# Whole key tiles for a sliding-window block and the first chunk of a memory-augmented attention, with a third token-major buffer

## The chip, the cores and the metric

The kernel runs on one core of one Trainium2 chip. Time is device microseconds of one execution; of several executions the median is taken. The core has five engines that run their own instruction streams and wait for one another through semaphores: TensorE (PE in the profile, its weight loads PEld), VectorE (DVE), ScalarE (ACT), GpSimd (POOL) and SyncE (SP), which here only issues DMAs. Each engine works its instructions in the order in which they were written.

## The reference

Two attentions on different inputs of 2048 tokens with 640 features, 32 heads of 20; the outputs stand side by side (2048 x 1280).

```python
# A: four segments of 512 tokens, in order, with a memory (M, z)
logits = q_s @ k_s.T * scale + mask           # causal inside the segment
a_dot  = softmax(logits) @ v_s
a_mem  = (phi(q_s) @ M) / (phi(q_s) @ z + 1e-6)   # phi(t) = t+1 if t>0 else exp(t)
o      = g * a_mem + (1-g) * a_dot            # g = sigmoid(beta), per head
M, z   = M + phi(k_s).T @ v_s, z + sum(phi(k_s))
A      = concat(o) @ wo_A
# B: sliding window: key j counts for query i when 0 <= i-j < 256
B      = (softmax(where(window, q @ k.T * scale, -1e9)) @ v) @ wo_B
out    = concat([A, B], -1)
```

## The kernel before

Both attentions are cut into four chunks of 512 tokens, and the eight chunks run in the order A0, B0, A1, B1, ..., B3, numbered n = 0 to 7. The 32 heads stand in eight groups g of four, the heads of a group in four bands of 32 partitions. A chunk is worked in two halves of four groups; `phases` (L1067) pairs the first half of one chunk with the second half of the one before.

For each chunk, `qk_job` (L405) projects queries and keys, writes them to a scratch in device memory and reads them back spread out by heads; `v_job` (L593) projects the values, token-major, 21 columns a head of which the last is one, so that the value product yields the softmax's denominator too. `pq_job` and `pk_job` make phi of q and k for the memory through `phi` (L437): one exponential on ACT and two operations on DVE for each group of 128 rows. `dm_job` updates the memory.

Scores are made in batches (`score_batch`, L680). A batch is up to 512 columns of queries for each of a group's four heads, with 128 keys on the partitions, in two banks of PSUM. An entry (kt, b0, nb, c0) means: key tile kt, against nb query blocks of 64 from block b0, at column c0. Two exponentials on ACT (L725) turn the two banks into the probability tile `pt` (six buffers, `NPT`). Where a key tile lies on the edge of the window, a mask follows: `mask` (L761) on GpSimd with an affine select, "diag" for the causal edge (L775) and "far" for the window's far edge (L771).

Before the change a diagonal is cut finer than a key tile: the tables `MAIN_A`, `MAIN_B` and `MAIN_B0` (L60 to L65) hold the whole tiles, and a further "half" batch pairs 64 keys with 64 queries (L692 to L710), two such squares stacked on the 128 partitions. Its mask is one DVE operation, `mask_half` (L748, L756). For the value product of such a half, the values of the other 64 keys must be zero: `v_job` copies half tiles of the values by DMA into the zero-padded tiles `vtop` and `vbot` (`vz`, L633 to L653; for the last half in the room of kA and qA, cleared by `clear_spare`). Per pair of groups A has four main batches of 512 columns and a half batch of 256. B has, per pair, four of 512 and a half batch of 512; in B's first chunk two of the main batches have 256. In the last chunk (n = 7) `unit` (L939) goes by query tile i: two batches of 512 and a half batch of 256 for each i and half.

The value product (`av`, L780) gathers a group's result of all queries in one PSUM bank of two; `turn` transposes it on DVE (L812), `norm` (L816) divides by the denominator (L835, L830) into the token-major tile `o` of the chunk (two buffers, L1301). `back_job` (L872) transposes `o` on DVE (L867) into `oD` (two buffers), after the output of chunk n-2 is done; `final_job` (L890) multiplies oD by the output weights, per 128 tokens in two pieces of 320 columns (L905), and stores 640 columns by a DMA (L919). In A's later chunks a second result, that of the memory, is added to o on GpSimd (L848).

The order of all of it is written out by a planner when the kernel is built. `Flow` (L75) keeps an estimated clock for each engine. The loop in `body` (L1158) takes, at each point, the next score batch if its inputs and banks are there, else a value product that is ready, else a projection job, and last an output projection (`fins`). A chunk's first value product asks that the tile `o` be free: `done.get((n-2, "oD"))` (L1206, L1211, L1227). `ORDER` holds a number for each batch that breaks ties, `SHIFT` how the two halves of a phase interleave, `T_W` when the first weights are expected. `evac` (L216) decides for each PSUM bank whether ACT (L224) or DVE (L226) copies it out: ACT if its estimated end lies before that of DVE less `EDGE`.

Of the kernel before, what the change touches and what calls it, by code (L numbers as in the profile page):

```python
# [9 lines left out]
ALU = mybir.AluOpType  # L10
# [3 lines left out]
P = 128  # L14
# [14 lines left out]
    713, 960, 766, 330, 869, 772, 401, 0, 661, 621, 0, 421, 799, 434, 873, 66, 0, 0, 682, 989,  # L29
    286, 308, 0, 611, 753, 150, 129, 90, 788, 0, 206, 866, 667, 116, 549, 871, 639, 130, 0, 0,  # L30
    912, 958, 43, 481, 0, 273, 464, 759, 0, 576, 75, 116, 453, 298, 776, 822, 0, 592, 326, 352,
    83, 232, 230, 0, 831, 0, 447, 297, 432, 523, 968, 587, 614, 386, 789, 692, 822, 229, 935,
    581, 834, 344, 0, 0, 113, 0, 549, 887, 906, 0, 610, 0, 343, 660, 0, 585, 0, 505, 0, 324, 0,
    71, 0, 0, 0, 312, 359, 655, 958, 400, 526, 773, 865, 950, 534, 3, 0, 753, 384, 394, 707,
    67, 758, 381, 953, 225, 83, 144, 0, 183, 598, 460, 507, 727, 0, 122, 0, 0, 568, 356, 711,
    739, 632, 0, 572, 339, 542, 0, 276, 229, 0, 0, 278, 631, 350, 717, 0, 0, 325, 609, 541,
    789, 0, 15, 479, 188, 0, 0, 688, 196, 403, 0, 956, 270,
)
STRETCH = 1
EDGE = -300.0  # L40
# [5 lines left out]
T_W = (5600.0, 7200.0, 10500.0, 12500.0, 14500.0, 16500.0)  # L46
SLACK = 500.0
SPREAD = 500.0
SHIFT = (0.0, 1.0, 0.75, 1.0, -0.5, 0.25, -1.0, 0.0, 0.0)
PKT = (2000.0, 2100.0, 1000.0)  # L50
NU = 2
SPREAD_NS = 400.0
# [13 lines left out]


# [122 lines left out]
class _K:  # L190
# [53 lines left out]
    def consts_rows(self):  # L244
# [17 lines left out]
        for kind, sides in (("A", ((0, -1, 0), (64, -1, 0))), ("B", ((0, -1, 0), (64, 1, -1)))):  # L262
# [174 lines left out]
    def phi(self, out, x, ready, then):  # L437

        nc, f = self.nc, self.f
        e = self.wk.tile([P, L], BF16, name="e", bufs=2)  # L440
        nc.scalar.activation(out=e[:], in_=x, func=ACT.Exp)  # L441
        ta = f.on_act(519.0, ready)

        def s1():
            nc.vector.tensor_scalar(out=out, in0=x, scalar1=1.0, scalar2=1.0,
                                    op0=ALU.add, op1=ALU.max)
            f.on_dve(150.0, 0.0, True)

        def s2():
            nc.vector.tensor_tensor(out=out, in0=out, in1=e[:], op=ALU.min)  # L450
            f.on_dve(345.0, 0.0, True)
# [4 lines left out]
    def phi_all(self, pieces, then):  # L456
# [6 lines left out]
        for x, (o_, i_) in enumerate(pieces):  # L463
            while len(ends) < x - 1:
                yield self.f.pe + 200.0
            if x > 1:
                yield ends[x - 2]

            def fin(x=x):
# [953 lines left out]
```

## Time and profile before

| what | value |
|---|---|
| median of 8 runs | 360.04 us (355.71 to 362.17) |
| the profiled execution | 360.22 us |
| its span, first to last instruction | 358.5 us |
| TensorE clock granted, mean | 0.995 |
| busy: PE, DVE, ACT, POOL | 332.9, 296.1, 316.7, 153.6 us |
| exponentials of scores (L725) | 328, of which 264 with 1024 elements and 64 with 512 |
| masks on GpSimd (L771, L775) | 184, each of 512 elements, 128.0 us |
| DMA engines busy on the main queue | 47.5% of the span |

How to read it: busy time of an engine is the union of its instructions' spans; since ACT's and PE's instructions overlap, the mean duration of one times their count is more than the busy time. In a row of instructions, the first number after the line and shapes is busy time, the second the mean in ns of one, and what follows is the idle time just before them with what ended it. In a timeline row the first two numbers are start and length in us. In a table of stretches each engine has its busy us and its count of instructions. The chain of waits is followed back from the last instruction.

### The profile page before, as it was taken

What the parts mean: (1) busy time and instruction counts of PE and PEld (TensorE: products, weight loads), DVE (VectorE), ACT (ScalarE), POOL (GpSimd) and SP (SyncE); (2) the same over time, 40 slices, a digit from 0 to 9 for tenths busy, and PEclk for the clock granted to TensorE, in tenths of its full rate; (3) what the DMA queues carried; (4) which work ended last, traced back from release to release, by engine and by line L of the source; (5) the groups of instructions that cost most, each with busy time, mean ns of one, the idle gap of its engine ahead of it and who ended that gap; (6) DMA issues with size and microseconds to landing.
All of it is one profiled execution on the core that took longest, in us unless ns stands there. A gap on an engine that the chain in (4) does not pass through costs nothing.

```text
span 358.5 us, 17793 instructions
## 1 busy us (share of the span) xinstructions
PE 332.9 (93%) x7732; PEld 184.6 (51%) x7732; DVE 296.1 (83%) x607; ACT 316.7 (88%) x406; POOL 153.6 (43%) x243
## 2 busy tenths in 40 slices
PE   8799999999999999999899989979999999989896
PEld 3345545454445544565645445645565545656564
DVE  7567878599999899988897997299898899898784
ACT  2586996699999999999999999679999999999892
POOL 8120222243246434565337256015664356545641
PEclk9899999999999999999999999999999999999999
DMA  7994784356775641557665332562335323211012
GB/s 224 386 407 145 188 147 135 121 162 168 239 168 152 174 123 58 164 150 144 210 189 146 93 90 82 176 168 58 108 110 176 94 74 121 79 59 57 23 60 75
DMA packets 43350, 51.12 MB, mean 143 GB/s; under 512 B 12984, under 2 KB 38392, under 8 KB 43272
## 3 DMA queue, kind: packets, MB, share of 16 engines
q1 hardware_dynamic: 42696, 49.57, 47.5%
q8 instruction: 60, 0.98, 1.2%
q10 hardware_dynamic: 576, 0.42, 0.4%
q14 instruction: 18, 0.15, 0.2%
HBM read 24.91 MB, written 19.14 MB: 123 GB/s over the span
## 4 chain that ended last, share of the span: by engine, by line
PE 50%; ACT 21%; DVE 14%; issue 6%; DMA 6%; POOL 1%; ACTq 0%; SPq 0%; DVEq 0%; POOLq 0%
ACT pt L725 19%; PE m L422 17%; PE m L606 7%; PE m L789 7%; PE sc L714 7%; PE m L905 7%; DVE tt L812 4%; PE sc L704 3%; DMA wv_A<-in_A_wv_dram 2%; DVE o L830 2%; DVE st L226 2%; DMA scr_qA<-st 1%; DMA beta<-in_A_beta_dram 1%; PE m L347 1%; ACT e L441 1%
## 5 line engine op out<-in xcount | busy, mean ns | idle before, releaser
L725 ACT ACTIVATE pt<-sc 128x1024 bf16<-128x1024 f32 (+1 forms) x328 | 284.1, 981 | 16.9 <-PE sc L714 9.3
L775 POOL TENSOR_SCALAR_AFFINE_SELECT pt<-pt 128x512 bf16<-128x512 bf16 x128 | 89.1, 696 | 166.3 <-ACT pt L725 145.2
L812 DVE STREAM_TRANSPOSE tt<-m 128x512 f32<-128x512 f32 x88 | 62.0, 709 | 17.4 <-PE m L789 16.3
L771 POOL TENSOR_SCALAR_AFFINE_SELECT pt<-pt 128x512 bf16<-128x512 bf16 x56 | 38.9, 695 | 29.3 <-ACT pt L725 27.1
L226 DVE CAST st<-m 128x512 bf16<-128x512 f32 x57 | 38.9, 683 | 11.4 <-PE m L422 10.8
L606 PEld LDWEIGHTS <-xT 128*128 128x128 bf16 x400 | 32.8, 99 | 18.6 <-issue 4.9
L830 DVE TENSOR_TENSOR o<-tt,rr 128x320 bf16<-128x320 f32 x64 | 37.9, 595 | 0.9
L905 PEld LDWEIGHTS <-oD 128*128 128x128 bf16 x280 | 24.4, 97 | 19.1 <-issue 10.0
L905 PE MATMUL m<-wo_A,oD 128*128 128x320 bf16 x160 | 28.3, 300 | 3.2 <-DVE tt L812 2.1
L714 PE MATMUL sc<-qA,kA 32*128 32x64 bf16 (+3 forms) x640 | 29.3, 252 | 1.4 <-ACT pt L725 0.8
L714 PE MATMUL sc<-qB,kB 32*128 32x64 bf16 (+3 forms) x896 | 28.0, 221 | 2.7 <-issue 1.5
L606 PE MATMUL m<-wv_A,xT 128*128 128x320 bf16 (+2 forms) x200 | 27.9, 281 | 2.6 <-DMA wv_A<-in_A_wv_dram 2.4
L606 PE MATMUL m<-wBv,xT 128*128 128x320 bf16 (+2 forms) x200 | 27.4, 273 | 0.7 <-DVE tt L812 0.5
L867 DVE STREAM_TRANSPOSE oD<-o 128x512 bf16<-128x512 bf16 x35 | 22.7, 676 | 5.9 <-PE m L905 5.9
L422 PE MATMUL m<-xT,wBk 128*128 128x512 bf16 x100 | 26.3, 380 | 1.1 <-DVE tt L812 0.5
L422 PE MATMUL m<-xT,wBq 128*128 128x512 bf16 x100 | 26.2, 381 | 0.5 <-DVE tt L812 0.2
L226 DVE CAST ot<-m 128x320 bf16<-128x320 f32 x48 | 22.6, 476 | 4.5 <-PE m L905 4.3
L789 PE MATMUL m<-pt,vB 128*32 128x64 bf16 (+3 forms) x896 | 23.4, 225 | 2.0 <-ACT ot L224 1.1
L714 PEld LDWEIGHTS <-kB 32*128 32x128 bf16 x896 | 13.4, 92 | 20.2 <-issue 19.2
L422 PE MATMUL m<-xT,wk_A 128*128 128x512 bf16 x90 | 22.8, 380 | 0.9 <-DVE st L226 0.7
L422 PE MATMUL m<-xT,wq_A 128*128 128x512 bf16 x90 | 22.3, 380 | 0.8 <-DVE tt L812 0.6
L789 PE MATMUL m<-pt,vA 128*32 128x64 bf16 (+3 forms) x640 | 21.8, 253 | 1.1 <-DVE ot L226 0.9
(106 smaller groups left out, 480.2 us busy)
## 6 DMA issues: line engine op xcount, KB each, us to landing
out_dram<-ot SPq DMA_DIRECT2D x31, 160.0 KB
scr_kB<-st SPq DMA_DIRECT2D x20, 128.0 KB
scr_qB<-st SPq DMA_DIRECT2D x20, 128.0 KB
kB<-scr_kB SPq DMA_DIRECT2D x32, 80.0 KB
qB<-scr_qB SPq DMA_DIRECT2D x32, 80.0 KB
scr_kA<-st SPq DMA_DIRECT2D x18, 128.0 KB
scr_qA<-st SPq DMA_DIRECT2D x18, 128.0 KB
kA<-scr_kA SPq DMA_DIRECT2D x28, 80.0 KB
```

The lines of the kernel that those rows point to most:

```text
L226: nc.vector.tensor_copy(out=out, in_=in_)
L422: nc.tensor.matmul(ps[:, :], lhsT=w_ap[:, kt, m * P:(m + 1) * P], rhs=xT[:, kt, :], start=(kt == 0), stop=(kt == self.KT - 1))
L606: nc.tensor.matmul(ps[:, c0:c0 + w], lhsT=xT[:, kt, tt * P:(tt + 1) * P], rhs=w_ap[:, kt, a:a + w], start=(kt == 0), stop=(kt == self.KT - 1))
L714: nc.tensor.matmul(ps[j // 2][:, j % 2, c0:c0 + 64 * nb], lhsT=k[rows, g, P * kc:P * kc + P], rhs=q[rows, g, 64 * b0:64 * (b0 + nb)], star ...
L725: nc.scalar.activation(out=pt[:, 2 * i:2 * i + 2, 0:hi], in_=ps[i][:, :, 0:hi], func=ACT.Exp, scale=self.scale)
L771: nc.gpsimd.affine_select(out=blk, in_=blk, pattern=[[0, r], [-1, w]], compare_op=ALU.is_ge, fill=self.zero, base=-1, channel_multiplier=1)
L775: nc.gpsimd.affine_select(out=blk, in_=blk, pattern=[[0, r], [1, w]], compare_op=ALU.is_ge, fill=self.zero, base=128 - w, channel_multipli ...
L789: nc.tensor.matmul(O[HD * j:HD * j + HD, c:c + 64 * nb], lhsT=self.vcols(v, h // 16 if vk[0] == "v" else 0, vt, h, HD), rhs=rhs[j], start= ...
L812: self.nc.vector.transpose(out=tt[:], in_=O[:, :])
L830: nc.vector.tensor_tensor(out=out, in0=a, in1=b, op=ALU.mult)
L867: self.nc.vector.transpose(out=self.oD[n][:, x:y, b0:b0 + nb, :].rearrange("p c b t -> p b c t"), in_=o[:, b0:b0 + nb, :].rearrange("p b ( ...
L905: nc.tensor.matmul(ps[:, 0:320], lhsT=oD[:, m, :, :].rearrange("p b t -> p (b t)"), rhs=wo[:, m, cs], start=(m == 0), stop=(m == self.KT - 1))
```

## The change

Four things go together.

1. For all B chunks and for A's first chunk (`WHOLE`) the scores go by whole key tiles of 128 x 128 alone. The half batches, their DVE mask and the zero-padded value copies are left out there; masks are 128 columns wide, on GpSimd. A's chunks 1 to 3 keep their halves. The batches per pair of groups: A0 five of 512 columns; B0 four of 512 and one of 256; B1 and B2 six of 512; B3 three of 512 for each query tile and half.
2. The tiles vtop and vbot of B are gone, and `o` has three buffers; a chunk's value products wait for oD of chunk n-3.
3. `phi` takes up to three groups in one instruction (`EW`), with one buffer for the exponentials (`EB`).
4. `final_job` makes, of 512 tokens, four pieces of 128 tokens x 512 columns and one piece with the remaining 128 columns of all four, each with a store of its own; the last chunk has `last_job` with two pieces of 320 columns for each 128 tokens, each stored on its own.

With these, `EDGE` goes from -300 to 250, `T_W`'s third entry from 10500 to 12300, `SPREAD_NS` from 400 to 540, and `ORDER` and `SHIFT` have other numbers.

```diff
-EDGE = -300.0
+EW, EB = 3, 1
+EDGE = 250.0
...
-T_W = (5600.0, 7200.0, 10500.0, 12500.0, 14500.0, 16500.0)
+T_W = (5600.0, 7200.0, 12300.0, 12500.0, 14500.0, 16500.0)
...
-SHIFT = (0.0, 1.0, 0.75, 1.0, -0.5, 0.25, -1.0, 0.0, 0.0)
+SHIFT = (0.0, 0.5, 0.0, 0.25, 0.0, 0.25, 0.5, 1.0, 0.0)
...
+WHOLE = ((0, 0), (0, 1), (1, 0), (1, 1), (3, 0), (3, 1), (5, 0), (5, 1), (7, 0), (7, 1))
+WHOLE_A = [([(0, 0, 8, 0)], [("diag", 0, 0, 128)]),
+           ([(3, 6, 2, 0), (1, 2, 6, 128)], [("diag", 0, 128, 128)])]
+WHOLE_B = [([(0, 0, 6, 128), (3, 6, 2, 0)], [("diag", 0, 128, 128), ("far", 384, 0, 128)]),
+           ([(1, 2, 6, 0), (-2, 0, 2, 384)], [("diag", 0, 0, 128), ("far", 256, 128, 128)]),
+           ([(2, 4, 4, 0), (-1, 0, 4, 256)], [("diag", 0, 0, 128), ("far", 384, 0, 128)])]
+WHOLE_B0 = [([(3, 6, 2, 0), (0, 0, 6, 128)], [("diag", 0, 128, 128), ("far", 384, 0, 128)]),
+            ([(2, 4, 2, 0), (1, 2, 6, 128)], [("diag", 0, 128, 128), ("far", 384, 0, 128)])]
...
-    def phi(self, out, x, ready, then):
+    def phi(self, out, x, w, ready, then):
...
+        e = self.wk.tile([P, EW, L], BF16, name="e", bufs=EB)[:, 0:w, :]
+        nc.scalar.activation(out=e, in_=x, func=ACT.Exp)
...
+        if (n, half) not in WHOLE:
+            t = yield from self.v_copies(n, half, v, gate, t)
+        for g in range(4 * half, 4 * half + 4):
+            self.mark(t + DVE_OUT, n, "v", g)
...
+    def final_job(self, n, wo, out2d, col):
+        nc, f = self.nc, self.f
+        yield self.known(n, "oD")
+        r = self.row0[n]
+        for x in range(LT + 1):
...
+            for y, (qt, a, w) in enumerate([(x, 0, 512)] if x < LT else
+                                           [(qt, 512, P) for qt in range(LT)]):
...
+            t = self.evac(ot[:], ps[:, :], 512, 612.0)
...
+                if (n, half) in WHOLE:
+                    for g in gs[::2]:
+                        out.append([n, [(g1, (i - y, 2 * i, 2, 256 * x + 128 * (2 - y)))
+                                        for x, g1 in enumerate((g, g + 1)) for y in (2, 1)],
+                                    [("far", 0, 256, 128)], []])
+                    out.insert(1, [n, [(g, (i, 2 * i, 2, 128 * x)) for x, g in enumerate(gs)],
+                                   [("diag", 0, 256, 128), ("diag", 128, 256, 128)], []])
...
+        if (n, half) in WHOLE:
+            for g0 in gs[::2]:
+                out = []
+                for g in (g0, g0 + 1):
+                    for ent, ms in WHOLE_A if kind == "A" else WHOLE_B if c else WHOLE_B0:
+                        out.append([n, [(g, e) for e in ent], ms, []])
+                    if g > g0 or c and kind == "B":
+                        out[-1][3].append(g)
+                    elif kind == "A":
+                        out.append([n, [(g, (2, 4, 4, 0)), (g + 1, (2, 4, 4, 256))],
+                                    [("diag", 0, 256, 128)], [g]])
+                    else:
+                        out.append([n, [(g, (2, 6, 2, 0)), (g + 1, (2, 6, 2, 128))], [], [g]])
...
-                            self.done.get((n - 2, "oD")) if n > 1 else 0.0]
+                            self.done.get((n - 3, "oD")) if n > 2 else 0.0]
...
-            o_t[n] = self.big.tile([P, L // HD, GW], BF16, name="o", bufs=2)
+            o_t[n] = self.big.tile([P, L // HD, GW], BF16, name="o", bufs=3)
```

## The prediction

> **What bounds the kernel now.** I read the busy table by engine first, then stretches of ten microseconds, then ScalarE's (ACT's) instructions in order of time, and last its waits.
>
> ```profile
> PE 332.9 (93%) x7732; PEld 184.6 (51%) x7732; DVE 296.1 (83%) x607; ACT 316.7 (88%) x406; POOL 153.6 (43%) x243
> ```
>
> No engine is far behind another, so the average decides nothing. The stretches (engine busy us, then clock and DMA) do:
>
> ```profile
> 60.00:70.00 10.00, 9.50 (x210) 4.71 (x197) 6.64 (x14) 4.68 (x7) 0.63 (x2) 1.00 0.42 131
> 130.00:140.00 10.00, 9.41 (x221) 4.78 (x214) 9.82 (x24) 10.00 (x14) 3.69 (x6) 1.00 0.25 76
> 180.00:190.00 10.00, 9.73 (x208) 4.53 (x205) 9.32 (x21) 10.00 (x13) 4.02 (x6) 1.00 0.66 196
> 230.00:240.00 10.00, 8.17 (x209) 5.24 (x208) 7.10 (x15) 6.54 (x11) 0.66 (x1) 1.00 0.73 192
> 250.00:260.00 10.00, 9.79 (x253) 5.48 (x254) 8.71 (x15) 9.93 (x13) 6.38 (x10) 1.00 0.34 97
> ```
>
> The fourth number is ACT. From 70 to 220 and from 240 to 340 it is full (9.3 to 10.0); it starves in the first 40 us (15.6 us idle), in 60 to 70 and in 220 to 240 (5 us each), and after 350. ACT therefore sets the pace except in those holes. Its main work and the cadence of it:
>
> ```profile
> L725 ACT ACTIVATE pt<-sc 128x1024 bf16<-128x1024 f32 x264 | 251.1, 1062 | 12.8 <-PE sc L714 9.3 <-PE sc L704 1.5 <-POOL pt L771 0.5
> L725 ACT ACTIVATE pt<-sc 128x512 bf16<-128x512 f32 x64 | 36.2, 645 | 4.0 <-PE sc L704 4.0
> 180.98 15.72 ACT L725 ACTIVATE pt<-sc 128x1024 bf16<-128x1024 f32 x17
> ```
>
> Seventeen exponentials in a row last 15.72 us; less the last one's 1.03, that is 0.918 us each, below their own 1.06 because they overlap. The shortest of the two widths (1030 and 591 ns) differ by 0.439, so a short one costs 0.48. The hole at 225 to 234, first ACT, then VectorE (DVE):
>
> ```profile
> 223.16 1.98 ACT L725 ACTIVATE pt<-sc 128x1024 bf16<-128x1024 f32 x2
> 234.06 1.94 ACT L725 ACTIVATE pt<-sc 128x1024 bf16<-128x1024 f32 x2 [0.77 <-PE sc L714]
> ```
>
> ```profile
> 232.86 3.08 DVE L867 STREAM_TRANSPOSE oD<-o 128x512 bf16<-128x512 bf16 x5 [5.93 <-PE m L905]
> ```
>
> Exponentials stop for 9 us. In the code a chunk's first value product waits until chunk n-2 has been turned into oD (two token-major buffers); that turn waits for the output projection (L905) of n-4, which runs last in priority. All six probability buffers fill, and scores stop.
>
> **The change, term by term** (against the profiled execution, 360.2 us: span 358.5 and 1.7 around it; the median of the runs is 360.0).
>
> *More exponentials.* Per pair of head groups: first A chunk, its half batch of 2x512 elements becomes 2x1024, +0.88 us, four pairs; first B chunk, six long and four short become eight and two, +0.88, four pairs; B chunks 1 and 2, ten long become twelve, +1.84, eight pairs; last chunk, per query tile and half, two short become long, +0.88, eight times. In all 48 long more and 32 short fewer: 44.1 - 15.4 = **+28.7 us** of ACT. 5.3 of it (first A chunk, first half of B) lies in the holes before 86 us and costs nothing; without that cover it costs 5.3. The other **+23.4** falls where ACT is full.
>
> *Wide phi.* 32 exponentials become 13. Two in a row take 1.15 us, so 0.56 each against 0.43 for 512 elements at the slope above: 0.13 fixed, 19 times: **-2** on ACT and about -3 on DVE. The one buffer adds a wait only where a half has over three groups (once); the first store of a half goes later, the last, which releases the spread, hardly.
>
> *Evacuations.* The threshold in `evac` moves by 550 ns towards DVE; one ACT evacuation lasts 590 to 630 ns. ACT has 10.6 us of them in its full stretches (80 to 220, 240 to 340). DVE loses the half-tile masks of all B chunks and of the first A chunk:
>
> ```profile
> L756 DVE TENSOR_TENSOR pt<-pt,hmaskB 128x2048 bf16<-128x2048 bf16 x12 | 14.8, 1230 | 0.6 <-ACT pt L725 0.6
> L756 DVE TENSOR_TENSOR pt<-pt,hmaskA 128x1024 bf16<-128x1024 bf16 x16 | 11.0, 689 | 0.2 <-ACT pt L725 0.2
> L756 DVE TENSOR_TENSOR pt<-pt,hmaskB 128x1024 bf16<-128x1024 bf16 x8 | 6.1, 758 | 0.1
> ```
>
> That is 14.8 + 6.1 + 4x0.69 = 23.7 us, and 2.5 more from the output (64 casts of 476 ns become 35 of 690 and 8 of 476). It has room for all of them: **-10.6** (bounds 0 and -10.6).
>
> *Masks on GpSimd (POOL).* 184 masks of 512 elements become 136, and 92 of 1024 are added. The trace has none of that size: at least 0.70 us (a 512), at most 1.39 (two). The 64-element select (240 ns) and the 512 one (696) give a slope for 1.22, which I take as it comes from the same operation: 136x0.696 + 92x1.22 - 128 = +79 us of POOL (bounds +31 and +95), 64% busy: still no bound, but later by a mask at the end of the last chunk, where two in a row replace one DVE operation: **+1**. What is indirect is DVE:
>
> ```profile
> L830 DVE TENSOR_TENSOR o<-tt,rr x64: 446/492/1091, 34.1 to 352.7; 128x320 bf16<-128x320 f32 x64
> ```
>
> The worst case exceeds the best by 645 ns, one mask long. Means over minima of this, of u and of phi's two steps sum to 15.4 us. With masks drawn twice as long, such waiting grows as the sum of squared lengths (203 to 89): +14 us of DVE. So DVE ends at 296 - 24 - 3 - 2.5 + 12 (evacuations) + 14 = 293, as full as before; cost 0, bounds 0 and +8 if its delays hold PE's two banks.
>
> The Trainium skill (SBUF — State Buffer, "Who interferes with whom") says that VectorE and GpSimd share a pair of ports as an exclusive lock, held for the whole instruction. The 645 ns agree, and it speaks against this change. If by that rule each of the 88 o and u steps lost a whole long mask, DVE would gain 107 us instead of 14, end at 386 and bound the kernel some 25 us above the forecast; by the means it stays at 293.
>
> *Third token-major buffer.* The wait becomes n-3, long fulfilled. The 9 us without exponentials go: **-9**; the evacuations that ACT did in the hole move to DVE, idle there for 5.9. Late next is the turn to oD, still behind L905 with two oD buffers. If only displaced, -4.
>
> *No copies.* 26 copies on the SyncE (SP) queue go (22 B, 4 of the first A chunk); output pieces add about ten. In the chain of waits:
>
> ```profile
> 46.15 3.13 DMA vbotA<-vA
> ```
>
> ```profile
> PE m L606 <- DMA wv_A<-in_A_wv_dram: 2.4, 1, 2.4
> ```
>
> The second row, of the waits, is TensorE (PE) standing still at 11 us for a weight that T_W now expects at 12300 instead of 10500. Both lie in starved stretches: **-5.5** (bounds 0 and -5.5).
>
> *PE.* 2240 matmuls fewer at the same columns. A B group's value product takes 0.81 to 0.89 us in 56 matmuls; its 1536 columns at 0.232 per 512 are 0.70. Over all groups, with the scores, some 7 us less. Output projection 20x0.144 twice, against 20x0.232 and 20 narrow ones: no change. ACT waits for scores 9.3 + 1.5 + 4.0 us in all (the first two rows of exponentials): **-2** (bounds 0 and -7).
>
> Sum: 23.4 - 2 - 10.6 + 1 - 9 - 5.5 - 2 = -4.7, so 360.2 - 4.7 = **355.5 us**. ORDER and SHIFT also reorder everything; no row prices that, and I allow 4 us each way.
>
> **Rivals.** (1) Slower: ACT keeps its evacuations. Place: DVE in 110 to 220; longer masks hold its port operations, the planner sees DVE late and leaves casts on ACT. Price 10.6: 366. For it: DVE is at 93 to 98% in 130 to 150. Against: 24 us less masking. Past 363.8 when ACT keeps over 8.1 of the 10.6. (2) No change: the hole is displaced, since the deferred projection must still run before n-3's successor can turn: -4 for -9, so 360.5. For it: oD stays at two buffers and PE is 93% busy. (3) Better: PE's 7 us count fully and the hole at 60 to 70 (ACT idle 5.3) halves: 355.5 - 5 - 2.6 = 348. Against: that hole follows qB's way through memory, which is not changed. That the change fails to do what it says is possible only for the third buffer, and is (2).
>
> **Chances.** Forecast 0.44, (1) 0.24, (2) 0.21, (3) 0.11. With 4 us around each and 1% (about what a measurement of this kernel can tell) at 356.4 and 363.6: faster 0.47, same 0.27, slower 0.26. The range runs from between (3) and the forecast to past (1), leaving out 2 in 10: 347 to 369; the forecast's own is 351.5 to 359.5.
>
> **What would show it.** Right: exponentials x344 with 312 long; ACT casts in full stretches near zero; no gap over 3 us around the middle; POOL near 231 us with 92 masks near 1.2 us; DVE near 293. Wrong: ACT's total over 340 us, the gap in the next chunk instead, L830's mean above 0.8 us, or PE waiting for banks held by DVE casts.

## The result, and the profile after

The changed kernel takes 360.44 us (median of 22 runs, 359.96 to 362.85), the kernel before 359.33 (59 runs, 355.71 to 365.33). The ratio is **1.0052 (95% interval 1.0035 to 1.0070)**: half a per cent slower, small but beyond the noise. It is more than the quotient of the two medians (1.0031), and the granted clock can account for that. The changed kernel's runs have a median of 360.2 us at a clock of 0.998 or more and 361.6 at 0.994 or 0.995; the runs of the kernel before that stand beside the experiments have 358.2 at 0.999 or more and 359.7 at 0.995. At an equal clock the change costs some 2 us. The forecast was 355.5, its own range 351.5 to 359.5. The profiled execution took 360.04 us, 358.0 of it span, at a granted clock of 0.999.

The busy table of the page (busy us, share of the span, instructions):

```profile
span 358.0 us, 13242 instructions
PE 332.1 (93%) x5515; PEld 165.8 (46%) x5515; DVE 298.4 (83%) x558; ACT 325.9 (91%) x367; POOL 222.2 (62%) x282
```

TensorE (PE) shows 2217 matmuls fewer and is as busy as before (332.9). VectorE (DVE) has 2.3 us more, ScalarE (ACT) 9.2 more, GpSimd (POOL) 68.6 more. The groups by line, shapes apart (busy us, mean ns of one, then the idle time before them):

```profile
L717 ACT ACTIVATE pt<-sc 128x1024 bf16<-128x1024 f32 x312 | 291.8, 1058 | 11.3 <-PE sc L706 10.6
L717 ACT ACTIVATE pt<-sc 128x512 bf16<-128x512 f32 x32 | 18.1, 649 | 0.1
L767 POOL TENSOR_SCALAR_AFFINE_SELECT pt<-pt 128x1024 bf16<-128x1024 bf16 x60 | 68.0, 1139 | 39.9 <-ACT pt L717 39.7
L763 POOL TENSOR_SCALAR_AFFINE_SELECT pt<-pt 128x1024 bf16<-128x1024 bf16 x32 | 36.7, 1151 | 2.7 <-ACT pt L717 2.6
L822 DVE TENSOR_TENSOR o<-tt,rr 128x320 bf16<-128x320 f32 x64 | 41.1, 643 | 0.5
L822 DVE TENSOR_TENSOR u<-tt,rr 128x320 bf16<-128x320 f32 x24 | 16.2, 674 | 0.9 <-POOL o L840 0.5
```

The counts are those of the forecast: 312 long exponentials, 32 short, 92 masks of 1024 elements. The two divisions, o and u, take 643 and 674 ns now; before, at the same shapes, 595 and 526:

```profile
L830 DVE TENSOR_TENSOR o<-tt,rr 128x320 bf16<-128x320 f32 x64 | 37.9, 595 | 0.9
L830 DVE TENSOR_TENSOR u<-tt,rr 128x320 bf16<-128x320 f32 x24 | 12.6, 526 | 0.5 <-DVE rr L835 0.3
```

The same stretches as in the prediction (busy us of PE, PEld, DVE, ACT, POOL, then clock and DMA) and one more:

```profile
60.00:70.00 10.00, 9.35 (x177) 5.01 (x176) 9.43 (x18) 9.69 (x12) 7.06 (x8) 1.00 0.33 106
170.00:180.00 10.00, 8.12 (x131) 4.49 (x126) 9.70 (x17) 9.83 (x12) 9.32 (x11) 1.00 0.58 178
230.00:240.00 10.00, 8.47 (x155) 4.83 (x152) 8.83 (x18) 9.72 (x11) 7.02 (x10) 1.00 0.58 155
```

ACT starves neither in 60 to 70 (it had 4.68) nor in 230 to 240 (6.54): the hole in the middle is gone, and so is that before 70. In 170 to 180 ACT, DVE and POOL are all at 9.3 or more. One hole is left; ACT's instructions there, in order of time:

```profile
32.06 0.70 ACT L452 ACTIVATE e<-kA 128x512 bf16<-128x512 bf16 x1
34.70 1.48 ACT L452 ACTIVATE e<-st 128x1536 bf16<-128x1536 bf16 x1 [1.94 <-DVE pqA L461]
39.42 0.55 ACT L235 CAST vB<-m 128x460 bf16<-128x460 f32 x1 [3.24 <-PE m L619]
40.52 12.02 ACT L717 ACTIVATE pt<-sc 128x1024 bf16<-128x1024 f32 x13 [0.55 <-PE sc L706]
```

And the chain of waits, shares of the span by engine, first of the kernel before:

```profile
PE 50%; ACT 21%; DVE 14%; issue 6%; DMA 6%; POOL 1%; ACTq 0%; SPq 0%; DVEq 0%; POOLq 0%
```

then of the changed kernel:

```profile
PE 47%; DVE 25%; ACT 16%; issue 5%; DMA 3%; POOL 2%; SPq 0%; ACTq 0%; DVEq 0%; POOLq 0%
```

DVE went from 14 to 25% of the chain, ACT from 21 to 16%. The waits of PE (matmuls and weight loads, all rows added) for DVE went from 19.9 to 31.0 us.

**Where the time went.** I cut both traces at the first exponential of each phase. Stage 0 is the first half of A0, 1 the second half of A0 with the first of B0, and so on to 8, the second half of B3. The stages 3 to 6 are those in which B1 and B2 are worked.

| stage | before, us | after, us | difference | forecast |
|---|---|---|---|---|
| 0 and 1 (start) | 40.1 + 45.8 | 40.5 + 38.9 | -6.5 | -5.5 |
| hole at 225 (in stage 5) | 8.9 | 0 | -8.9 | -9 |
| 2 to 8 without the hole | 254.8 | 269.0 | **+14.2** | +8.8 |
| after the last exponential | 8.8 | 9.5 | +0.7 | +1 |

(The forecast's +8.8 is 23.4 - 10.6 - 2 - 2 + 0.) Three rows came out near the forecast, the first of them for another reason than the forecast's (see the start, below); the full stretches grew by 5.4 us too much. The experiments ask why. "The four stages" below are 3 to 6: 166.1 us before (with the hole of 8.9 in them), 169.6 after.

### The profile page after: what moved, and what is told of

Same layout as the page of the kernel before. It is cut to its first block, busy times and chain, and to the rows that moved or that the text cites. A ratio compares the mean times of both kernels' runs of the same rounds, so it can differ in the third digit from the quotient of the medians.

```text
span 358.0 us, 13242 instructions
## 1 busy us (share of the span) xinstructions
PE 332.1 (93%) x5515; PEld 165.8 (46%) x5515; DVE 298.4 (83%) x558; ACT 325.9 (91%) x367; POOL 222.2 (62%) x282
## 4 chain that ended last, share of the span: by engine, by line
PE 47%; DVE 25%; ACT 16%; issue 5%; DMA 3%; POOL 2%; SPq 0%; ACTq 0%; DVEq 0%; POOLq 0%
ACT pt L717 15%; PE m L433 14%; PE sc L706 8%; PE m L895 8%; PE m L781 7%; PE m L619 5%; DVE tt L804 4%; DVE oD L859 3%; DVE st L237 3%; DMA xT<-in_A_x_dram 2%; DVE o L822 2%; DVE vA L631 2%; DVE st L461 2%; DVE ot L237 2%; PE m L1057 2%
## 5 line engine op out<-in xcount | busy, mean ns | idle before, releaser
L717 ACT ACTIVATE pt<-sc 128x1024 bf16<-128x1024 f32 (+1 forms) x344 | 307.6, 1020 | 11.3 <-PE sc L706 10.6
L767 POOL TENSOR_SCALAR_AFFINE_SELECT pt<-pt 128x512 bf16<-128x512 bf16 (+1 forms) x148 | 128.0, 867 | 124.3 <-ACT pt L717 123.3
L763 POOL TENSOR_SCALAR_AFFINE_SELECT pt<-pt 128x512 bf16<-128x512 bf16 (+1 forms) x80 | 72.1, 902 | 2.7 <-ACT pt L717 2.6
L237 DVE CAST st<-m 128x512 bf16<-128x512 f32 x74 | 50.2, 680 | 14.1 <-PE m L433 12.6
L706 PE MATMUL sc<-qB,kB 32*128 32x128 bf16 (+2 forms) x928 | 42.7, 248 | 3.0 <-ACT pt L717 2.5
L619 PEld LDWEIGHTS <-xT 128*128 128x128 bf16 x400 | 32.4, 97 | 17.5 <-issue 7.6
L706 PE MATMUL sc<-qA,kA 32*128 32x64 bf16 (+4 forms) x608 | 30.1, 261 | 1.9 <-DVE qA L237 1.3
L237 DVE CAST ot<-m 128x512 bf16<-128x512 f32 (+1 forms) x39 | 25.3, 650 | 6.9 <-PE m L895 4.2
L895 PE MATMUL m<-wo_A,oD 128*128 128x512 bf16 (+1 forms) x160 | 26.0, 300 | 4.4 <-DVE vB L237 2.9
L895 PEld LDWEIGHTS <-oD 128*128 128x128 bf16 x280 | 19.6, 98 | 19.7 <-issue 8.2
L781 PE MATMUL m<-pt,vB 128*32 128x128 bf16 (+2 forms) x928 | 25.7, 250 | 1.9 <-DVE vA L631 0.6
L619 PE MATMUL m<-wBv,xT 128*128 128x320 bf16 (+2 forms) x200 | 26.6, 273 | 0.8 <-DVE tt L804 0.6
L619 PE MATMUL m<-wv_A,xT 128*128 128x320 bf16 (+2 forms) x200 | 26.2, 273 | 1.1 <-DVE vA L631 1.1
L781 PEld LDWEIGHTS <-vB 128*32 128x32 bf16 x928 | 17.6, 97 | 14.1 <-issue 4.6
L781 PE MATMUL m<-pt,vA 128*32 128x448 bf16 (+5 forms) x608 | 22.2, 264 | 1.2 <-DVE st L237 1.0
```

Source lines behind the costliest of these rows:

```text
L237: nc.vector.tensor_copy(out=out, in_=in_)
L619: nc.tensor.matmul(ps[:, c0:c0 + w], lhsT=xT[:, kt, tt * P:(tt + 1) * P], rhs=w_ap[:, kt, a:a + w], start=(kt == 0), stop=(kt == self.KT - 1))
L706: nc.tensor.matmul(ps[j // 2][:, j % 2, c0:c0 + 64 * nb], lhsT=k[rows, g, P * kc:P * kc + P], rhs=q[rows, g, 64 * b0:64 * (b0 + nb)], star ...
L717: nc.scalar.activation(out=pt[:, 2 * i:2 * i + 2, 0:hi], in_=ps[i][:, :, 0:hi], func=ACT.Exp, scale=self.scale)
L763: nc.gpsimd.affine_select(out=blk, in_=blk, pattern=[[0, r], [-1, w]], compare_op=ALU.is_ge, fill=self.zero, base=-1, channel_multiplier=1)
L767: nc.gpsimd.affine_select(out=blk, in_=blk, pattern=[[0, r], [1, w]], compare_op=ALU.is_ge, fill=self.zero, base=128 - w, channel_multipli ...
```

## The experiments

**1. Each engine's work raised by some 22 us in B1 and B2.** In the changed kernel: every fourth exponential twice, 19 of 32 long masks twice, the transposes of results twice, the score matmuls three times.

```diff
+            if i == 0 and n in (3, 5):                               # twice_act
+                self.twice = getattr(self, "twice", 0) + 1
+                if self.twice % 2:
+                    nc.scalar.activation(out=pt[:, 0:2, 0:hi], in_=ps[0][:, :, 0:hi],
+                                         func=ACT.Exp, scale=self.scale)
...
+        again = 1                                                    # twice_pool
+        if self.mask_n in (3, 5) and w * r == 1024:
+            self.twice = getattr(self, "twice", 0) + 1
+            again += self.twice * 19 // 32 > (self.twice - 1) * 19 // 32
...
+        if self.turn_n in (3, 4, 5):                                 # twice_dve
+            self.twice = getattr(self, "twice", 0) + 1
+            if self.twice > 1:
+                self.nc.vector.transpose(out=tt[:], in_=O[:, :])
...
-            for j in range(4):                                       # twice_pe
+            for j in [0, 1, 2, 3] * (3 if n in (3, 5) else 1):
```

> The changed kernel in its own order, with every second first exponential of B1 and B2 issued twice: 24 more exponentials of 1024 elements, 24 x 0.904 = 21.7 us more of ScalarE between 116 and 286 us, result unchanged. Theory (ScalarE's occupied time sets the length of these stages): 20 to 22 us longer, 381. Rival (TensorE sets it, 93% busy): ScalarE has about 2 us of idle time a stage, 8 us in all, so 12 us longer at most.

> The changed kernel in its own order, with 19 of the 32 masks of 1024 elements of B1 and B2 issued twice: 19 x 1.14 = 21.7 us more of GpSimd, result unchanged. Theory: GpSimd is 70% busy there and hidden, 0 to 3 us longer, 361 to 363. Rival (the masks, by their length and by the ports that VectorE shares, are what made stages 3 to 6 longer): 8 us or more.

> The changed kernel in its own order, with 31 of the transposes out of PSUM of B1, A2 and B2 issued twice: 31 x 0.709 = 22.0 us more of VectorE, result unchanged. Theory: VectorE has 4 to 7 us idle in each of these stages, but each second transpose also holds a PSUM bank of TensorE; 3 to 8 us longer, 363 to 368. Rival (VectorE became the bound after it took the casts): 15 us or more.

> The changed kernel in its own order, with the score products of B1 and B2 issued three times: 96 x 0.23 = 22 us more of TensorE, result unchanged. Theory: TensorE's busy time is mostly overlap, but its idle time is 2 to 4 us a stage, so much of it comes through: 8 to 15 us, 368 to 375, less than ScalarE's 20 to 22. Rival (TensorE sets the pace): 20 to 22 us, and ScalarE's less.

Measured: 380.72 us (ratio 1.0613, 1.0574 to 1.0651), 373.90 (1.0422, 1.0301 to 1.0544), 378.85 (1.0560, 1.0523 to 1.0598) and 372.16 (1.0374, 1.0342 to 1.0405). The surprise is that all four come through, ACT's 21.7 us with 20.3; for DVE and POOL my theories (3 to 8, and 0 to 3) fell. The four stages tell more than the totals. An engine's work cannot take longer than they last:

| kernel | four stages | PE | DVE | ACT | POOL |
|---|---|---|---|---|---|
| changed | 169.6 | 158.6 | 147.4 | 163.9 | 115.1 |
| twice_act | 189.3 | 166.2 | 144.0 | 187.3 | 113.6 |
| twice_pe | 181.8 | 177.8 | 142.7 | 167.5 | 114.6 |
| twice_dve | 187.3 | 158.4 | 167.9 | 166.1 | 114.7 |
| twice_pool | 180.7 | 162.9 | 148.6 | 165.0 | 134.5 |

ACT and PE had 5.7 and 11.0 us of room, so most of what they cost is plain overflow. DVE had 22.2 us of room, and its 22.0 us still cost 18.4; POOL had 54 and its 21.7 cost 13.5, or 10.2 at an equal clock (372.12 for 361.88, both at 0.994; the other of the two runs was granted 0.991). So room on the average of these stages is worth next to nothing to DVE and little to POOL: in the order written out, their operations stand between others that wait. (A second transpose also holds one of PE's banks for longer; how much of the 18.4 is that isn't split.)

**2. The third token-major buffer taken away.**

```diff
-            o_t[n] = self.big.tile([P, L // HD, GW], BF16, name="o", bufs=3)
+            o_t[n] = self.big.tile([P, L // HD, GW], BF16, name="o", bufs=2)
```
(and the value products wait for n-2 again)

> The changed kernel with two token-major buffers again (value products wait for chunk n-2), planned anew with the same ORDER. Theory (the third buffer removed the hole of 8.9 us without exponentials): a hole of 6 to 9 us comes back at the start of a chunk, 366 to 369. Rival (the hole was one of an unlucky plan, and the buffer does little): no gap over 3 us, 359 to 362.

Measured: 373.77 us (1.0426, 1.0370 to 1.0482). ACT's instructions in order of time there:

```profile
166.72 5.61 ACT L717 ACTIVATE pt<-sc 128x1024 bf16<-128x1024 f32 x6 [0.58 <-PE sc L706]
172.16 1.10 ACT L452 ACTIVATE e<-st 128x1024 bf16<-128x1024 bf16 x1
175.66 1.06 ACT L452 ACTIVATE e<-st 128x1024 bf16<-128x1024 bf16 x1 [2.40 <-DVE st L461]
178.49 0.54 ACT L235 CAST vB<-m 128x460 bf16<-128x460 f32 x1 [1.77 <-PE m L619]
183.78 0.58 ACT L235 CAST ot<-m 128x512 bf16<-128x512 f32 x1 [4.75 <-PE m L895]
184.86 0.58 ACT L235 CAST ot<-m 128x512 bf16<-128x512 f32 x1 [0.49 <-PE m L895]
187.59 0.58 ACT L235 CAST ot<-m 128x512 bf16<-128x512 f32 x1 [2.14 <-PE m L895]
188.07 4.70 ACT L717 ACTIVATE pt<-sc 128x1024 bf16<-128x1024 f32 x5
```

No exponential of scores (L717) starts between 172.2 and 188.1 us. The buffer does what the forecast says of it; the hole comes back a stage earlier and, in an order planned anew, longer than before (15.7 us for 8.9), so that the time went 5 us past my range.

**3. The casts given back to ACT, and the tie-breaking numbers set to zero.**

```diff
-EDGE = 250.0
+EDGE = -300.0
...
-ORDER = (
...
-)
+ORDER = (0,)
```

The first edit is edge_back, the second after_ties0 and, made in the kernel before, before_ties0.

> The changed kernel with EDGE at -300 again, planned anew: casts go back to ScalarE. Theory (ScalarE's occupied time decides, a cast costs it 0.47 or 0.31 us): about 17 casts in the full stretches, 6 to 8 us longer, 366 to 368. Rival (VectorE is as much a bound, 0.84 us for each us added to it in its own order): the two cancel, 359 to 362.

> The changed kernel with ORDER all zeros, so that the planner takes its first choice at every tie; work the same. It prices the written-out list. If the list is worth little, 360 to 364; if the plan hangs on it, 368 or more. No theory of the engines' work expects a difference.

> The kernel before with ORDER all zeros. Beside the same of the changed kernel it compares the two without their lists. Theory (15 us of exponentials paid, 17 us of holes saved): the holes of the kernel before stay, and the difference between the two is within 3 us, as with the lists. Rival (the list of one of them makes the result): they differ by over 5 us.

Measured: edge_back 371.38 us (1.0343, 1.0282 to 1.0404); its casts on ACT in stages 1 to 8 go from 1.9 to 16.6 us and these stages from 308 to 320.9. With ORDER neutral (SHIFT, EDGE and `T_W` stay) the changed kernel takes 2 us more (362.40, 1.0108, 1.0062 to 1.0155) and the kernel before 15 (373.91, 1.0423, 1.0375 to 1.0472). Without either list the changed kernel is 11.5 us the faster; with both it is 1.1 the slower. Part of this is the clock: the four runs of before_ties0 were granted 0.981 or 0.982, those of after_ties0 0.998 to 1.000. At the 1.4 us that the changed kernel loses from 0.998 or more to 0.995, some 5 of the 15 and of the 11.5 us go with it, an estimate; whether the order brings the lower clock about isn't shown. The rest, some 6 us, the kernel before has from its list.

**4. Half of the masks left out, and the hole at the start filled.**

```diff
+        part, rows = blk, r                                          # masks_half
+        if self.mask_n in (3, 5):
+            part, rows = blk[:, 0:blk.shape[1] // 2, :], r // 2
...
+            if n == 0 and len(self.sc_free) in (4, 6, 8, 10, 12, 14, 16):   # twice_act_start
+                nc.scalar.activation(out=pt[:, 2 * i:2 * i + 2, 0:hi], in_=ps[i][:, :, 0:hi],
+                                     func=ACT.Exp, scale=self.scale)
```

> The changed kernel in its own order, with the masks of B1 and B2 put on two of the four heads only, so that half of the masking there is left out: 32 masks go from 1.14 to about 0.69 us and 64 from 0.69 to about 0.45, 29 us less of GpSimd between 116 and 286 us. Theory (masks are hidden behind ScalarE, forecast cost 0): 0 to 2 us shorter. Rival (longer masks hold TensorE's value products and VectorE's port operations, as 13.5 us from 21.7 us of doubled masks suggests): 4 to 8 us shorter, and the stages 3 to 6 lose most of what they gained.

> The changed kernel in its own order, with seven of the first chunk's first exponentials issued twice, 6.3 us more of ScalarE before 33 us. Theory (what lies before 40 us is bound by the way of the second half's keys and queries through memory, and 8.3 us without exponentials stand before it): 0 to 1 us longer. Rival (the start is bound by ScalarE like the rest): 5 to 6 us longer.

masks_half: 357.29 us (0.9944, 0.9913 to 0.9975), and the four stages 165.7, that is -3.9. POOL has 28 us less there; DVE, whose instructions are the same, has 7.0 us less (140.4). The divisions again, then two stretches of ten microseconds:

```profile
L826 DVE TENSOR_TENSOR o<-tt,rr 128x320 bf16<-128x320 f32 x64 | 39.0, 609 | 0.5
L826 DVE TENSOR_TENSOR u<-tt,rr 128x320 bf16<-128x320 f32 x24 | 14.5, 604 | 0.9 <-POOL o L844 0.5
```

```profile
150.00:160.00 10.00, 9.26 (x131) 4.13 (x130) 8.59 (x18) 9.45 (x11) 7.01 (x14) 1.00 0.78 210
170.00:180.00 10.00, 9.40 (x138) 5.00 (x137) 9.15 (x19) 10.00 (x13) 7.82 (x12) 1.00 0.50 152
```

With POOL at 7.0 and 7.8, PE has 9.4 in 170 to 180 for 8.12 in the changed kernel. PE's waits for DVE in the whole kernel fall from 31.0 to 25.1 us. So the masks, which the forecast put at no cost, cost about 3.9 us in B1 and B2 alone. (POOL is still at 87.2 us in the four stages, for 75.9 before the change.) Whether they cost it through DVE's slower operations or through value products that wait for a mask isn't split.

twice_act_start: 369.76 us (1.0272, 1.0211 to 1.0332), 9.3 us for 6.3 of work. Its four runs were granted 0.991 to 0.995; the one at 0.995 (368.46) lies 6.9 us above the changed kernel's median at that clock (361.55). So all of the 6.3 comes through, and what is above it may be the clock. The hole of 8.0 us is still there, at 40.8 to 48.8: it moved behind the added work instead of taking it in. The projections that end it stand behind the first half's scores in PE's queue: L619's start at 41.3 us, after the last scores, which waited for ACT until 38.1.

**5. Other orders, and the last half in half batches again.**

```diff
-EDGE = 250.0                                # new_order, with another ORDER
+EDGE = 600.0
-T_W = (5600.0, 7200.0, 12300.0, 12500.0, 14500.0, 16500.0)
+T_W = (5600.0, 7200.0, 13500.0, 14500.0, 11500.0, 16500.0)
-SHIFT = (0.0, 0.5, 0.0, 0.25, 0.0, 0.25, 0.5, 1.0, 0.0)
+SHIFT = (1.0, 0.5, 1.0, 0.25, 0.0, 0.0, 0.25, 1.0, -0.5)
...
-WHOLE = ((0, 0), (0, 1), (1, 0), (1, 1), (3, 0), (3, 1), (5, 0), (5, 1), (7, 0), (7, 1))
+WHOLE = ((0, 0), (0, 1), (1, 0), (1, 1), (3, 0), (3, 1), (5, 0), (5, 1), (7, 0))
```

The second edit, with `clear_spare` and its copies back, is last_halves (an order of its own, EDGE 150) and last_halves_own (the changed kernel's numbers).

> The changed kernel with the same parts, another order alone: other numbers in ORDER and SHIFT, EDGE 600 for 250, T_W's third to fifth entries 13500, 14500, 11500 for 12300, 12500, 14500. No work is added or taken away. My theory: the full stretches are set by the exponentials that whole tiles add (some 21.6 us of ScalarE) and by the port waits of VectorE behind longer masks, and no order takes either away; an order can only shorten the ScalarE hole at 32 to 40 us and single waits, 0 to 3 us in all, so 357.5 to 360.5, ratio to before 0.995 to 1.005. Rival: the lost gain was an unlucky order, that is the list of the changed kernel was as far from its best as the neutral list is from the old one (15 us); then 352 or below, ratio under 0.985.

> The changed kernel, but the second half of the last chunk takes its diagonals in half batches again (the copies in the room of kA and qA with them), and an order of its own in ORDER, SHIFT, EDGE (150) and T_W. Eight of the 48 exponentials that went from 512 to 1024 elements or were added go back: 4 times 0.88 = 3.5 us of ScalarE, and 8 masks of 1024 elements leave GpSimd for VectorE, all in the last 60 us. My theory (exponentials cost 0.94 of their cadence where ScalarE is full, and a run of masks at the very end of the kernel is not hidden): the last two stages and the end together, 72 us in the changed kernel, fall by 3 to 4 us, and the whole comes 2 to 4 us below the kernel with a new order alone: 354 to 357.5. Rival: at the end of the kernel it is not ScalarE but the chain of value products, transposes and stores that counts; then those stages stay at 71 to 73 us and the time is that of the kernel with a new order, within 1 us.

> The changed kernel with the second half of the last chunk in half batches again, as in the run before, but with the changed kernel's own numbers in ORDER, SHIFT, EDGE and T_W. 4 x 0.88 = 3.5 us of ScalarE go. If exponentials cost 0.94 there: the last two stages and the end, 72.1 us in the changed kernel, come to 68 to 69.5, and the time to 356 to 358. Rival (the last stages are a chain of value products, transposes and stores): within 1 us of the changed kernel, 359.5 to 361.

Measured: 362.38 us (1.0101, 1.0068 to 1.0135), 360.06 (1.0029, 1.0007 to 1.0050) and 361.32 (1.0035, 1.0005 to 1.0064). One other order is no better, which speaks against the rival of an unlucky one, and I missed my own range for it by 2 us. The third run is the telling one: stages 7, 8 and the end, 72.1 us in the changed kernel, have 3.5 us of exponentials less and take 71.1. I had expected 68 to 69.5. At the end, too, exponentials taken away are hardly time gained, and nothing of it is left in the total (361.38 for 361.55, the medians at 0.995).

**6. As much ACT work taken away as the change added there, and the wide phi undone.**

```diff
+            if n in (3, 5) and self.twice % 2:                       # thin_act: both of every second batch
+                nc.scalar.activation(out=pt[:, 2 * i:2 * i + 2, 0:hi].bitcast(F32),
+                                     in_=ps[i][:, :, 0:hi // 2], func=ACT.Exp, scale=0.0)
...
-EW, EB = 3, 1                                                        # narrow_phi
+EW, EB = 1, 2
```

> The changed kernel, but in B1 and B2 both exponentials of every second batch read 512 score columns instead of 1024 and write a constant over the same bytes of the probability tile (part of the softmax is left out). 48 instructions shorter by 0.904 - 0.478 = 0.426 us each: 20.4 us less ScalarE work in the four stages from the second half of A1 to the first half of A3, about what whole tiles added there; scores, masks, value products and their order stay. My theory (every engine is a link; ScalarE the tightest, and TensorE is next with 158.6 of the 169.6 us of these stages): the first half of the gain counts, then TensorE and VectorE bind: 8 to 14 us off, 346 to 352. Rival A (ScalarE alone sets the pace, as the forecast's sum takes it): 0.94 x 20.4 = 19 off, 341. Rival B (the longer masks or TensorE set the pace, and the added exponentials were hidden): less than 5 off, 355 or more.

> The changed kernel with phi as before: EW, EB = 1, 2 for 3, 1, so 32 exponentials of 512 elements for 13 wider ones, and as many more pairs of steps on VectorE. The forecast's term for the wide phi was -2. If it is right, 19 x 0.13 = 2.5 us of ScalarE come back at 0.94, and VectorE gets 3 us more at its measured 0.84: 362 to 365. Rival: the wide phi was worth nothing, since its one buffer and its late first store take back what the fixed parts give: 359.5 to 361.5.

thin_act: 359.03 us (0.9971, 0.9943 to 0.9999), 1.4 us under the changed kernel, or 2.9 by the two ratios. ACT's busy time in the four stages falls by 18.1 us, to 145.8, and they take 168.5 instead of 169.6. The wait of ACT's exponentials for PE's scores in that window (us in total, times, longest), thin_act:

```profile
ACT pt L723 <- PE sc L706: 17.9, 28, 1.8
```

and the changed kernel:

```profile
ACT pt L717 <- PE sc L706: 4.7, 12, 1.1
```

Most of what ACT saves, it waits for scores. My theory (8 to 14 us off) falls, and so does the forecast's premise that ACT sets the pace.

narrow_phi: 368.36 us (1.0246, 1.0189 to 1.0302), 7.9 us slower, or 6.4 at a clock of 0.995 (two runs, 367.9 and 368.0, for 361.55), for a term that the forecast put at 2. ACT has 4.5 us more and DVE 4.8 (303.2). The forecast had not counted DVE's part. The order is written anew with it, so not all of this need be phi's.

**7. Cuts put together.** With the cut of thin_act: half the masks too (thin_both), EDGE at -300 (thin_edge), or two of five matmuls left out of the projections of A2, B2 and A3 (thin_pe).

```diff
+                if n not in (4, 5, 6) or kt not in (2, 3):           # thin_pe, in qk_job and v_job
                     nc.tensor.matmul(...)
```

> The changed kernel with two cuts together, both in B1 and B2: the 48 exponentials of 512 read columns (18 us of ScalarE; part of the softmax is left out) and the masks on two of four heads (29 us of GpSimd, and so 7 us of port waits of VectorE; half of the masking is left out). Alone the first took about 1 to 3 us off and the second 3 to 4. New theory (two chains of nearly equal length: ScalarE's exponentials, and TensorE with VectorE through two banks; with ScalarE cut the second stays, with VectorE cut the first): together they give clearly more than their sum, the stages from the second half of A1 to the first half of A3 go from 169.6 (168.4 and 165.7 with one cut) to 160 or below, the whole to 348 to 353. Rival (no second chain, only single waits that each cut shortens): the sum of the two, 354.5 to 356.5.

> The kernel with EDGE at -300 (371.4, where ScalarE has 14.7 us more casts and 169.7 busy of 176.1 in the four stages) with the same 48 exponentials cut to 512 read columns, part of the softmax left out. In the changed kernel this cut of 18 us moved the end by 1 to 3 us. If with EDGE at -300 ScalarE alone is the longer chain, the same cut takes 7 to 12 us off: 359 to 364. If the casts cost through the order and through TensorE's banks, not through ScalarE's fullness: 368 or more.

> The kernel with the 48 exponentials of 512 read columns (359.0 us), and with two of the five matmuls of each projection group left out for A2, B2 and A3 (q, k and v; part of the projections is left out): 60 matmuls of 512 columns at 0.216 us and 48 of 320 columns' worth at 0.14, 19.7 us less TensorE work between 80 and 285 us, in the same written order. ScalarE has 22.6 us idle in the four stages there. If TensorE sets the pace (155 busy of 168.4 us, the rest short waits for VectorE), at least 0.6 of it comes through: 341 to 348. If it is VectorE with the written order and the two banks: less than 6 us off, 353 or more.

thin_both 356.28 us (0.9892, 0.9843 to 0.9940): 4.2 us under the changed kernel, no more than its parts, so my theory of two chains falls. thin_edge 369.72 (1.0263, 1.0211 to 1.0315): the same cut gives 1.7 us there, so the casts on ACT do not cost edge_back its 11 us because ACT is full; that it is by where they stand is argued, not shown. thin_pe 360.88 (1.0042, 1.0002 to 1.0082): no gain over thin_act's 359.03 as it stands, and far from the 12 us that I had put on a pace set by PE. But the two were not granted the same clock: thin_act's ten runs had 0.995 to 1.000, thin_pe's, without the slowest, 0.976 to 0.995, and the lower the slower, from 357.78 at 0.995 to 362.49 at 0.976. At 0.995, with one run each, thin_pe took 2.6 us less than thin_act (360.35). Its trace has two stretches in the four stages with half the clock, the last number but two:

```profile
195.40:198.80 3.40, 3.07 (x21) 1.21 (x19) 1.36 (x3) 1.09 (x2) 2.63 (x4) 0.50 0.17 47
239.80:243.20 3.40, 3.40 (x26) 1.01 (x29) 2.63 (x5) 1.67 (x3) 2.29 (x3) 0.50 0.40 128
```

That is at most 3.4 us of lost PE time. In the four stages:

| kernel | four stages | PE | DVE | ACT | POOL |
|---|---|---|---|---|---|
| thin_act | 168.5 | 155.1 | 147.5 | 145.8 | 116.7 |
| thin_both | 164.9 | 155.1 | 140.3 | 145.9 | 88.5 |
| thin_pe | 169.1 | 143.9 | 148.3 | 145.5 | 116.7 |

Of the cuts at a full clock only that of the masks, with DVE's time, clearly moves the length; what thin_pe's matmuls are worth, 0 to some 3 us, lies within its clock. Stretches of five microseconds of thin_pe (columns as above):

```profile
150.00:155.00 5.00, 3.71 (x56) 1.66 (x40) 4.84 (x11) 3.90 (x6) 5.00 (x7) 1.00 0.69 168
160.00:165.00 5.00, 4.53 (x129) 2.22 (x122) 3.86 (x8) 4.94 (x7) 1.32 (x2) 1.00 0.28 88
175.00:180.00 5.00, 3.27 (x51) 1.54 (x53) 4.97 (x9) 3.64 (x6) 5.00 (x6) 1.00 0.52 172
190.00:195.00 5.00, 2.46 (x32) 1.38 (x32) 4.97 (x11) 4.11 (x6) 4.80 (x7) 1.00 0.39 113
```

In three of them POOL and DVE are full while PE and ACT have room; in the other it is ACT, and POOL stands still. No engine is full over the four stages, but nearly every few microseconds one is. I counted it: the four stages in pieces of 2.5 us, and in how many an engine is busy for over 98%.

| kernel | pieces | PE | DVE | ACT | POOL | none |
|---|---|---|---|---|---|---|
| before | 66 | 41 | 21 | 49 | 3 | 6 |
| changed | 67 | 39 | 25 | 52 | 23 | 3 |
| masks_half | 66 | 44 | 19 | 54 | 4 | 4 |
| thin_pe | 67 | 12 | 28 | 29 | 23 | 9 |

POOL, at 68% of these stages (115.1 of 169.6), is full in a third of the pieces; before the change it was in 3 of 66.

## Why the prediction was wrong

**The step that failed** is the one on the masks: "64% busy: still no bound", and for DVE "as full as before; cost 0, bounds 0 and +8 if its delays hold PE's two banks". It was made from averages of the whole kernel. The instruction price was right (1.22 us forecast, 1.14 to 1.15 measured; POOL 222 for 231 us; DVE 298 for 293), and the mechanism was named, in the bound and in the list of what would show it wrong, though the sign given there, a mean of the division above 0.8 us, did not come (0.643). But the masks come in runs, one batch after another, and fill POOL in 23 of 67 pieces; beside them DVE's divisions take 643 and 674 ns instead of 595 and 526, and PE waits 11.1 us more for DVE. Halving them in two chunks brought 3.9 us in the four stages (3.2 in the total), where the forecast had 0; the full stretches missed by 5.4. The masks of A0, B0 and B3 were not tried.

The Trainium skill (SBUF — State Buffer, "Who interferes with whom") calls the ports that VectorE and GpSimd share an exclusive lock. The runs agree in the direction, 643 and 674 ns against 609 and 604 with fewer masks; a whole long mask lost by each division, the reading that the prediction weighed, is not seen.

**The premise** "ACT therefore sets the pace except in those holes" fell as well. Its terms, +23.4 for exponentials and -10.6 for casts, gave nearly the right sum (12.8 of the 14.2) without ACT being what makes the length: 18.1 us of ACT work taken out of the four stages brought 1.1 us of their length, and casts put back cost as much with ACT thinned as without. What ACT's additions cost (20.3 for 21.7) does not tell what its savings bring. An engine at 163.9 of 169.6 us is overrun at once by more work, and freed of work it waits for the next.

**Third buffer**: right in place and size, -9 forecast, -8.9 in the stage table, and two_o brings the gap back (it costs 13.3 us there, in a new order). Its rival, that the gain is displaced, is neither shown nor excluded. In the hole of the kernel before PE was busy throughout:

```profile
225.10:234.06 8.96, 8.96 (x127) 5.95 (x129) 2.35 (x5) 5.48 (x13) 0.80 (x1) 1.00 0.65 192
```

That work is still to be done: PE has 156.7 us in the four stages before and 158.6 after. But thin_pe, with 143.9, still takes 169.1, at most 3.4 of them by its clock, so PE's work alone does not account for it.

**Start**: -5.5 forecast, -6.5 measured: the size is right, by luck. The forecast's two waits, at 11 and at 46 us, were to go; the first did, and still nothing was gained up to stage 1 (40.1 before, 40.5 after), and the second lay in no starved stretch (ACT was busy for 9.68 of the 10 us from 40 to 50). The gain is all in stage 1, 45.8 to 38.9, where a hole of 8.0 us that the forecast left standing is gone. ACT before (two rows, with casts alone between them) and after:

```profile
55.23 3.77 ACT L725 ACTIVATE pt<-sc 128x1024 bf16<-128x1024 f32 x4 [0.34 <-PE sc L714]
66.96 2.92 ACT L725 ACTIVATE pt<-sc 128x1024 bf16<-128x1024 f32 x4
```

```profile
40.52 23.45 ACT L717 ACTIVATE pt<-sc 128x1024 bf16<-128x1024 f32 x26 [0.55 <-PE sc L706]
```

The hole is absent from two_o, edge_back, narrow_phi and after_ties0 too, so it is neither the third buffer nor EDGE, the wide phi or ORDER alone that removed it; what did is open. Part of the 6.5 may be the clock, of which the trace before was granted half from 14.6 to 18.0 us. That added exponentials hide in a hole is not borne out either: twice_act_start paid for all of its 6.3 us.

**End**: +1 forecast, +0.7 measured. **Wide phi**: mis-sized, -2 for up to -6.4 or -7.9 (DVE's 3 us were set down and not counted); how much of it is the new order isn't split. **PE**: the credit of 2 is not seen; fewer matmuls left its busy time at 332.1 for 332.9. **Order**: the 4 us allowed each way hold for new_order (+1.9); no row could have told that the list of the kernel before was worth some 10 to 15 us.

**The rivals.** "ACT keeps its evacuations" did not come (8 casts left of 44). The number is that of the second rival, 360.5, but not its mechanism as far as the trace shows: no gap over 3 us is left around the middle. Of the third, the half about the hole at 60 to 70 came true, and more than that.

**Sums of the prediction that do not come out.** ACT is not full as far as 340 us (8.40 from 330 to 340). Waiting of 15.4 us that grows from 89 to 203 grows by 19.7, not 14, which puts DVE at 298, where it was measured. A DVE of 386 us would lie 30 us above the forecast, not 25. And the four chances, with 4 us around each as the standard deviation of a normal spread, give 0.40, 0.37 and 0.23 for faster, same and slower, not 0.47, 0.27 and 0.26: the outcome that came was rated too low.

**What stays open.** Of the 14.2 us in the full stretches the masks of B1 and B2 are shown, 3.9. The other ten, for which the forecast had 8.8, are not split among exponentials, casts, PE's displaced work and the order; a cut does not give back what an addition costs (ACT: 1.4 us for 18.1 taken away, 20.3 for 21.7 added). A cut of DVE's own work, and thin_pe with short masks, which would tell whether POOL's runs or DVE hold the stages, were not tried. No version that computes everything was faster than the kernel before.

## What to carry to other kernels

Where four engines are between 60 and 95% busy, cut the full stretches into pieces of a few operations and count in how many each engine is full: an average of 68% hid an engine that was full in a third of them. Price additions and savings apart, since a stretch that lengthens with every engine's additions may shorten little with the savings of most; take a cost away on the chip before a gain is put on it. And where an order hangs on tie-breaking numbers, compare the parts with these numbers neutral too: here they were worth 15 us to one kernel (some 5 of them with a lower clock) and 2 to the other. Before a version is called no faster, compare its granted clock.

## What the runs showed that I had not expected

- With nothing else changed in DVE's instructions, 28 us less of GpSimd masks took 7.0 us off DVE's busy time in the same four stages.
- Idle time at a hole does not take in work put before it: 6.3 us of exponentials ahead of an 8 us hole cost 6.9 us at an equal clock, and the hole moved whole.
- Four stages kept their length (169.1 us for 169.6, at most 3.4 of them by a halved clock) with 18.4 us less ScalarE and 14.7 us less TensorE busy time in them (thin_pe against the changed kernel).
- The kernel with fewer matmuls was granted less of the clock than the one in the same order with all of them: 0.976 to 0.995 in nine of thin_pe's ten runs, 0.995 to 1.000 in thin_act's. Over these nine its time went from 357.78 to 362.49 us.
- A mask of 1024 elements takes 1.14 us where one of 512 takes 0.70: by the element the long mask is the cheaper, and yet the masks of the changed kernel fill GpSimd for whole pieces, as those before hardly did (3 of 66).
